# The MLP's tokens in three blocks of 128 and a doubled rest of 64, whose mixing products run as pairs in the row halves

## The chip, the cores and the metric

One core of a Trainium2 chip runs the whole program. Its engines have queues of their own and meet at semaphores: TensorE (PE, with its weight loads as PEld), VectorE (DVE), ScalarE (ACT), GpSimd (POOL) and SyncE (SP), which issues most DMAs. The metric is the device time of one execution in microseconds.

## The reference: what is computed

Three layers on 4 batches of S = 448 tokens with 768 channels:

```
scores = cap * tanh(scale * q @ k.T / cap);  x = softmax(scores) @ v        # 12 heads of 64
out += mask[e] * w[e] * causal_attention(x @ wq[e], x @ wk[e], x @ wv[e]) @ wo[e]   # 4 experts, 2 chosen per token
h = gelu(x @ w_in);  u, v = h[..., :512], h[..., 512:]                       # the MLP
v_n = layer_norm(v) * g_ln
v_s = einsum('ts,bsd->btd', w_sg, v_n) + b_sg                                # mixes the tokens
out = x + (u * v_s) @ w_out
```

The change is in the MLP: in v, its norm, and the mixing product with w_sg over the 448 tokens.

## The kernel before

Products that need more than one pass of precision are made of a high and a low part, rounded to fp32r: hi*hi + hi*lo + lo*hi, three matmuls per slice. A matmul of plain f32 is two records in the trace, one of fp32r a single one (the trace prints f32 for both on PE). The first 48 slots hold the 12 heads of each batch, with the experts of the batch before beside them; there the program order is pinned on every engine (`keep_in_program_order`, and `pin` for PE). Behind them `pe_pin[0] = False`: PE's matmuls of the last part, from some 280 us on, are ordered by the scheduler, by its own estimate of when each can run, and the other engines follow. That last part holds the experts of batch 3 (tiles qk3, a3, pe3, tr3, pt3, v3), the ends of batch 2's (tr2, av2) and the whole MLP, interleaved by `together`:

- `mlp_a(b)` (L858): yh, yl are the high and low part of the MLP's input, channels on partitions (128 x 2 x 448). For each of NC = 4 chunks of CP = 112 tokens, 6 matmuls give hv (tokens x 512 in one PSUM bank); `gelu2` (ACT and DVE, with two buffers of `tmp`) gives vg, DVE takes mean and variance, POOL the power (rstd), and vh, vl (112 x 4 x 512) are the normed v in two parts.
- `mlp_b(b)` (L892): for each f of 4 slices of 128 features, `up(f)` gives u from 6 matmuls hu, and `gate(f)` the mixing sp: 4 chunks x 3 matmuls that contract over 112 tokens each, 448 columns wide; DVE scales and gates it (vs), ACT rounds gh, DVE takes the rest gl.
- `mlp_c(b)` (L936): six slices m of the output o, 18 matmuls each (6 from y, 12 from gh and gl).
- `mlp_weights`: loads and rounds w_sg (sg_h, sg_l, in the same chunks of 112), w_out in thirds, and wo (wo_h, wo_l), wu_h, wu_l.

`tmp` (L806) is a ring of 6 buffers of 128 x 512, `ps` five PSUM banks for hv, hu, sp and o. A matmul whose operands lie in 64 partitions (64*112 and 64*128 in the rows) uses one row half of the array; so do the products a of the experts (two heads, one in each half: a3_0_0_2 and a3_0_1_2 are blocks 2 of heads 0 and 1 of expert pair 0) and s of the attention. av runs in column halves (112*64).

Of the kernel before, what the change touches and what calls it, by code (L numbers as in the profile page):

```python
# [10 lines left out]
F32 = mybir.dt.float32  # L11
# [16 lines left out]
FH = FF // 2  # L28
# [46 lines left out]
def build(ctx: ExitStack, tc: tile.TileContext, a: dict):  # L75
# [44 lines left out]
    def mm(*args, **kw):  # L120
        pin(nc.tensor.matmul(*args, **kw))  # L121
# [669 lines left out]
    w2 = ES(tc.tile_pool(name="w2", bufs=1, side="right", reuse_waits="tile"))  # L791
    ml = ES(tc.tile_pool(name="ml", bufs=1, side="right", reuse_waits="tile"))
    ps = ES(tc.tile_pool(name="ps", bufs=5, space=PSUM, side="right", reuse_waits="tile"))
    sg_h = w3.tile([CP, NC, S], F32R, name="sg_h")
    sg_l = w3.tile([CP, NC, S], F32R, name="sg_l")
    gln = w3.tile([128, 4], F32, name="gln")
    bsg = w3.tile([128, S], F32, name="bsg")
    mhalf = w3.tile([CP, 1], F32, name="mhalf")
    w2_h = w2.tile([128, 2, FF], F32R, name="w2_h")
    w2_l = w2.tile([128, 2, FF], F32R, name="w2_l")  # L800
    wu_h = wp.tile([128, 4, DM], F32R, name="wu_h", tag="wa")
# [2 lines left out]
    wo_l = wp.tile([128, 2, DM], F32R, name="wo_l", tag="wb")  # L804

    def tmp(name):  # L806
        return ml.tile([128, 512], F32, tag="tmp", name=name, bufs=6)

    def mlp_weights(part):
        if part == 1:  # L810
            yield from more_weights()
            return
        if part == 2:
            for i in range(3):
                yield from w_out(3, i, 3, *[lambda dt, name: ml.tile([128, 512], dt, tag="tmp", name=name, bufs=6)] * 2, by="a")
            return
        for k in range(2):
            nc.sync.dma_start(w2_h[:, k, :].bitcast(F32), w2_d[0][:, k, :])
            nc.sync.dma_start(w2_l[:, k, :].bitcast(F32), w2_d[1][:, k, :])
        nc.sync.dma_start(gln, a["g_ln"])  # L820
        nc.sync.dma_start(bsg, a["b_sg"].to_broadcast([128, S]))
        dve.memset(mhalf, -0.5)
        for k in range(NC):
            t = tmp(f"w_sgT{k}")[:CP, :S]
            nc.sync.dma_start(t, a["w_sgT"][:, k, :])
            rnd("pav"[int(GA) % 10], sg_h[:, k, :], t)
            rest("pv"[int(GA) // 10], sg_l[:, k, :], t, sg_h[:, k, :])
        yield 1.0
# [29 lines left out]
    def mlp_a(b):  # L858
        while b == 1 and B - 1 not in X:
            yield 500.0  # L860
        yh, yl = (pool.tile([128, 2, S], F32R, tag=tag, name=f"y{t}{b}", bufs=n)
                  for t, (pool, tag, n) in zip("hl", y_places[b]))
        rnd("v", yh, YA[b])
        rest("p" if YL else "v", yl, YA[b], yh)
        pool, *tags = v_places[b]
        vh = pool.tile([CP, NC, FH], F32R, tag=tags[0], name=f"vh{b}")
        vl = pool.tile([CP, NC, FH], F32R, tag=tags[1], name=f"vl{b}")
        for c in range(NC):
            g = ps.tile([128, 512], F32, tag="g", name=f"hv{b}_{c}")
            n = 0  # L870
            for k in range(2):
                ck = slice(c * CP, (c + 1) * CP)
                for x, w in ((yh, w2_h), (yh, w2_l), (yl, w2_h)):
                    mm(g[:CP, :], x[:, k, ck], w[:, k, FH:], start=(n == 0), stop=(n == 5))
                    n += 1
            yield 1278.0
            vg = tmp(f"vg{b}_{c}")[:CP, :]
            gelu2(vg, g[:CP, :], CP, FH, f"v{b}_{c}")

            bs = ml.tile([CP, 6], F32, tag="bs", name=f"bs{b}_{c}", bufs=2)  # L880
            dve.bn_stats(bs, vg)
            mv = ml.tile([CP, 2], F32, tag="mv", name=f"mv{b}_{c}", bufs=2)
            dve.bn_aggr(mv, bs)
            rstd = ml.tile([CP, 1], F32, tag="rstd", name=f"rstd{b}_{c}", bufs=2)
            dve.tensor_scalar(rstd, mv[:, 1:2], 4e-6, None, op0=ALU.add)
            pool_e.tensor_tensor(rstd, rstd, mhalf, op=ALU.pow)
            dve.tensor_scalar(vg, vg, mv[:, 0:1], rstd, op0=ALU.subtract, op1=ALU.mult)
            rnd("a", vh[:, c, :], vg)
            rest("p" if c < SL else "v", vl[:, c, :], vg, vh[:, c, :])
        st[b] = (yh, yl, vh, vl)  # L890

    def mlp_b(b):  # L892
        yh, yl, vh, vl = st[b]
        pool, *tags = g_places[b]
        gh, gl = ([pool.tile([128, S], F32R, tag=tag, name=f"g{t}{b}_{f}", bufs=4) for f in range(4)]
                  if tag[:2] == "pe" else
                  columns(pool.tile([128, 4, S], F32R, tag=tag, name=f"g{t}{b}"))
                  for t, tag in zip("hl", tags))
        us = {}

        def up(f):
            g = ps.tile([128, 512], F32, tag="g", name=f"hu{b}_{f}")
            n = 0
            fk = slice(f * 128, (f + 1) * 128)
            for k in range(2):
# [92 lines left out]
def _layout(x):  # L998
    q, k, v = x["q"], x["k"], x["v"]
    wide = lambda w: w.transpose(1, 0, 2).reshape(DM, E * HD)  # L1000
    wo = x["moe_wo"].reshape(E * HD, DM)
    out = {
        "qT": q.reshape(B, HP, 2, S, D).transpose(0, 2, 4, 1, 3).reshape(B, 2 * D, HP, S),
        "kT": k.reshape(B, HP, 2, S, D).transpose(0, 2, 4, 1, 3).reshape(B, 2 * D, HP, S),
        "v": v[:, :, :KB * 128].reshape(B, H, KB, 128, D).transpose(0, 3, 1, 2, 4),
        "vt": v[:, :, KB * 128:].reshape(B, HP // 2, 2, 2, KT, D).transpose(0, 1, 2, 4, 3, 5).reshape(B, HP // 2, 2 * KT, 2, D),
        "wqk": _rows(np.concatenate([wide(x["moe_wq"]), wide(x["moe_wk"])], 1)),
        "wvg": _rows(np.concatenate([wide(x["moe_wv"]), x["moe_w_gate"]], 1)),
        "wo": _rows(wo),
        "woT": _rows(wo.T),  # L1010
        "w_in": _rows(x["moe2_w_in"]).view(np.int64),
        "w_out": _rows(x["moe2_w_out"]).view(np.int64),
        "w_sgT": x["moe2_w_sg"].T.reshape(NC, CP, S).transpose(1, 0, 2),
        "g_ln": x["moe2_g_ln"].reshape(4, 128).T,
        "b_sg": x["moe2_b_sg"].reshape(1, S),
    }
# [12 lines left out]
    return {n: np.ascontiguousarray(w) for n, w in out.items()}
# [17 lines left out]
```

## Time and profile before

| | |
|---|---|
| median of 3 runs | 529.7 us (528.77 to 530.01) |
| the profiled execution | 528.26 us |
| its span | 526.5 us |

The page shows busy times, the span in 40 slices, DMA queues, and the chain of work that ended last, followed back from the last instruction. The rows that matter stand below. A duration of a matmul is modelled and overlaps the next one; what one costs in a row of many is the distance from start to start.

### The profile page before, as it was taken

The page shows a single profiled execution, that of the slowest core. Times are in us where ns is not written, and L with a number is a line of the kernel's source. Part 1 is how long each engine was busy: PE and PEld are TensorE (multiplying, and loading weights), DVE is VectorE, ACT ScalarE, POOL GpSimd, SP SyncE. Part 2 cuts the span into 40 slices and gives each one's busy share as a digit, 9 for nine tenths or more (in the row PEclk, how much of TensorE's full clock was granted, in tenths as well). Part 3 has the DMA queues.
Part 4 walks back from the last instruction along what each step waited for, and adds up shares of the span by engine and source line. Part 5 has one row for each costly group of instructions (what it writes and reads, how often), then busy time and mean ns, then how long its engine had stood idle before and what let it go on. Part 6 is the DMA issues. An engine that isn't in the chain of part 4 may idle for free.

```text
span 526.5 us, 7575 instructions
## 1 busy us (share of the span) xinstructions
PE 509.7 (97%) x2726; PEld 333.6 (63%) x2726; DVE 331.0 (63%) x693; ACT 320.8 (61%) x532; POOL 111.7 (21%) x134
## 2 busy tenths in 40 slices
PE   7999999999999999999999999999899999999997
PEld 2233333455655555555466758878778899899996
DVE  4999998974467546465774698838424795483300
ACT  7989899788777776768652675633444363352211
POOL 0000000161451341441340716009030010010000
PEclk9999999999999999999999999999899999999999
DMA  8965529553514232440129312200620001001111
GB/s 317 336 214 162 186 60 244 168 170 112 150 60 149 56 114 84 114 97 13 34 79 269 76 40 71 71 1 12 229 89 17 2 0 54 35 34 38 36 59 63
DMA packets 34693, 54.16 MB, mean 103 GB/s; under 512 B 5536, under 2 KB 29536, under 8 KB 34656
## 3 DMA queue, kind: packets, MB, share of 16 engines
q1 hardware_dynamic: 33936, 50.31, 31.0%
q0 software_dynamic: 576, 3.15, 1.7%
q8 instruction: 21, 0.34, 0.3%
q10 hardware_dynamic: 144, 0.23, 0.1%
q14 instruction: 16, 0.13, 0.1%
HBM read 41.92 MB, written 11.75 MB: 102 GB/s over the span
## 4 chain that ended last, share of the span: by engine, by line
PE 70%; DVE 13%; ACT 6%; DMA 4%; issue 3%; POOL 3%; SPq 1%; DVEq 0%; POOLq 0%; ACTq 0%
PE o L121 16%; PE po L121 8%; PE s L121 8%; PE qk L121 7%; PE sp L121 7%; PE v L121 5%; PE hv L121 4%; ACT p L106 4%; PE a L121 3%; PE hu L121 3%; PE av L121 3%; PE tr L539 3%; DVE pb L106 3%; DMA rb<-rd 2%; POOL pe L106 1%
## 5 line engine op out<-in xcount | busy, mean ns | idle before, releaser
L106 ACT ACTIVATE p<-s,tsc 128x896 f32<-128x896 f32 x84 | 80.9, 1006 | 19.1 <-PE s L121 18.8
L121 PE MATMUL s<-qp,kp 64*128 64x448 f32 (+1 forms) x384 | 78.1, 566 | 2.7 <-ACT p L106 2.7
L106 ACT ACTIVATE p<-p,capt 128x1792 f32<-128x1792 f32 (+1 forms) x48 | 76.9, 1603 | 1.1
L106 DVE TENSOR_TENSOR pb<-pb,p 128x896 f32<-128x896 f32 (+1 forms) x48 | 53.2, 1109 | 19.7 <-ACT p L106 10.5
L106 POOL TENSOR_TENSOR pb<-p 128x896 f32<-128x896 f32 x14 | 29.9, 2134 | 167.1 <-PE po L121 93.5
L121 PE MATMUL po<-p,vv 128*64 128x448 f32 x288 | 59.4, 548 | 0.0
L121 PEld LDWEIGHTS s<-qp,kp 64*128 64x128 f32 (+1 forms) x384 | 27.2, 173 | 47.6 <-issue 24.0
L106 DVE CUSTOM_DVE_ANT_0 a<-a,neg 112x112 f32<-112x112 f32 (+3 forms) x64 | 28.1, 463 | 35.1 <-PE a L121 34.6
L106 POOL TENSOR_SCALAR pe<-pe,cs 112x112 f32<-112x112 f32 (+1 forms) x64 | 37.8, 615 | 57.6 <-DVE cs L106 57.6
L106 ACT ACTIVATE pe<-a,m 112x112 f32<-112x112 f32 (+3 forms) x64 | 31.3, 494 | 19.8 <-DVE m L106 18.3
L121 PEld LDWEIGHTS po<-p,vv 128*64 128x64 f32 x288 | 18.5, 136 | 37.9 <-issue 34.7
L121 PE MATMUL qk<-xh,wqk_h 128*128 128x448 f32 x96 | 37.2, 389 | 0.1
L106 ACT ACTIVATE ob<-o 128x448 f32<-128x448 f32 x24 | 13.0, 541 | 37.8 <-PE o L121 37.8
L121 PE MATMUL o<-gh,wu_h 128*128 128x448 f32 x96 | 35.8, 373 | 0.0
L121 PE MATMUL o<-gl,wu_h 128*128 128x448 f32 x96 | 35.8, 372 | 0.0
L121 PE MATMUL qk<-xh,wqk_l 128*128 128x448 f32 x96 | 35.2, 366 | 0.0
L121 PE MATMUL o<-gh,wu_l 128*128 128x448 f32 x96 | 34.8, 368 | 0.0
L539 PE MATMUL tr<-ident,pe 112*112 112x112 f32 x160 | 25.9, 266 | 6.7 <-ACT pe L106 2.5
L106 POOL TENSOR_TENSOR rstd<-rstd,mhalf 112x1 f32<-112x1 f32 x16 | 10.2, 635 | 102.3 <-DVE rstd L106 98.9
L106 ACT ACTIVATE pt<-tr 112x112 f32<-112x112 f32 (+3 forms) x48 | 18.8, 404 | 17.2 <-PE tr L539 16.9
L121 PE MATMUL v<-wvg_h,xh 128*112 128x260 f32 x96 | 28.5, 296 | 0.1
L539 PEld LDWEIGHTS tr<-ident,pe 112*112 112x112 f32 x160 | 18.3, 135 | 14.5 <-issue 8.8
(228 smaller groups left out, 1097.5 us busy)
## 6 DMA issues: line engine op xcount, KB each, us to landing
rb<-rd SPq DMA_DIRECT2D x24, 224.0 KB, 5.8
out_dram<-ob SPq DMA_DIRECT2D x24, 224.0 KB, 1.9
kp<-in_kT_dram SPq DMA_DIRECT2D x23, 224.0 KB, 3.1
qp<-in_qT_dram SPq DMA_DIRECT2D x23, 224.0 KB, 3.3
vv<-in_v_dram SPq DMA_DIRECT2D x24, 192.0 KB, 3.4
wuw<-in_w_out_dram SPq DMA_DIRECT2D x6, 384.0 KB, 3.4
wud<-wuw SPq DMA_DIRECT2D x12, 192.0 KB, 1.9
ws<-in_wqk_dram SPq DMA_DIRECT2D x4, 384.0 KB, 6.4
```

The lines of the kernel that those rows point to most:

```text
L106: ins = f(*args, **kw)
L121: pin(nc.tensor.matmul(*args, **kw))
L539: pin(nc.tensor.transpose(g[:CP, j * CP:(j + 1) * CP], pe[:, j * CP:(j + 1) * CP], ident))
```

## The change

The tokens are cut into 3 blocks of 128 and a rest of 64 (KB = 3, KT = 64) instead of 4 chunks of 112. The rest is stored twice, in partitions 0 to 63 and 64 to 127. To get v so, the last 64 columns of yh and yl are copied twice side by side into yrh, yrl (DVE, two copies per batch), which are the stationary operand of the fourth hv. w_sg is laid out likewise in DRAM, its last 64 rows twice. The mixing of one f is then 9 matmuls of 128 rows (`mixed`) and three of 64 rows (`rests`), which are issued for f and f + 1 in turns, f in the lower row half and f + 1 in the upper. The gates of f and f + 1 follow both. tmp has 5 buffers instead of 6.

```diff
-    sg_h = w3.tile([CP, NC, S], F32R, name="sg_h")
-    sg_l = w3.tile([CP, NC, S], F32R, name="sg_l")
+    sg_h = w3.tile([128, KB + 1, S], F32R, name="sg_h")
+    sg_l = w3.tile([128, KB + 1, S], F32R, name="sg_l")
...
-        return ml.tile([128, 512], F32, tag="tmp", name=name, bufs=6)
+        return ml.tile([128, 512], F32, tag="tmp", name=name, bufs=5)
...
-        for k in range(NC):
-            t = tmp(f"w_sgT{k}")[:CP, :S]
+        for k in range(KB + 1):
+            t = tmp(f"w_sgT{k}")[:, :S]
...
+        rh, rl = (ml.tile([128, 2, 2, KT], F32R, tag=f"yr{t}", name=f"yr{t}{b}", bufs=1) for t in "hl")
+        for r, y in ((rh, yh), (rl, yl)):
+            dve.tensor_copy(r, y[:, :, KB * 128:].unsqueeze(2).to_broadcast([128, 2, 2, KT]))
+        last = {id(yh): rh, id(yl): rl}
         pool, *tags = v_places[b]
-        vh = pool.tile([CP, NC, FH], F32R, tag=tags[0], name=f"vh{b}")
-        vl = pool.tile([CP, NC, FH], F32R, tag=tags[1], name=f"vl{b}")
-        for c in range(NC):
+        vh = pool.tile([128, KB + 1, FH], F32R, tag=tags[0], name=f"vh{b}")
+        vl = pool.tile([128, KB + 1, FH], F32R, tag=tags[1], name=f"vl{b}")
+        for c in range(KB + 1):
             g = ps.tile([128, 512], F32, tag="g", name=f"hv{b}_{c}")
             n = 0
             for k in range(2):
-                ck = slice(c * CP, (c + 1) * CP)
                 for x, w in ((yh, w2_h), (yh, w2_l), (yl, w2_h)):
-                    mm(g[:CP, :], x[:, k, ck], w[:, k, FH:], start=(n == 0), stop=(n == 5))
+                    ck = (x[:, k, c * 128:(c + 1) * 128] if c < KB else
+                          last[id(x)][:, k].rearrange("p t q -> p (t q)"))
+                    mm(g, ck, w[:, k, FH:], start=(n == 0), stop=(n == 5))
                     n += 1
...
-        def gate(f):
+        def mixed(f):
             g = ps.tile([128, 512], F32, tag="g", name=f"sp{b}_{f}")
-            n = 0
             fk = slice(f * 128, (f + 1) * 128)
-            for c in range(NC):
+            for c in range(KB):
                 for x, w in ((vh, sg_h), (vh, sg_l), (vl, sg_h)):
-                    mm(g[:, :S], x[:, c, fk], w[:, c, :], start=(n == 0), stop=(n == 3 * NC - 1))
-                    n += 1
+                    mm(g[:, :S], x[:, c, fk], w[:, c, :], start=(c == 0 and w is sg_h and x is vh), stop=False)
+            return g
+
+        def rests(gs):
+            for x, w in ((vh, sg_h), (vh, sg_l), (vl, sg_h)):
+                for f, g in gs.items():
+                    r = slice(64 * (f % 2), 64 * (f % 2) + 64)
+                    mm(g[:, :S], x[r, KB, f * 128:(f + 1) * 128], w[r, KB, :], start=False, stop=x is vl)
+
+        def gate(f, g):
...
-        for f in range(4):
-            if f < 3:
-                up(f + 1)
-                yield 1120.0
-            gate(f)
-            yield 2240.0
+        for f in (0, 2):
+            gs = {}
+            for t in (f, f + 1):
+                if t < 3:
+                    up(t + 1)
+                    yield 1120.0
+                gs[t] = mixed(t)
+                yield 1830.0
+            rests(gs)
+            for t, g in gs.items():
+                gate(t, g)
+            yield 610.0
```

The scheduler lays out PE's last part anew from this. Three places of its order, each as it stands before and after. Number behind a name: the instruction's own.

PE in batch 0, where the mixing of f = 2 ends, before (sp0_2 is the mixing of batch 0, f = 2; tr are transposes of the experts):

```order
L121 MATMUL sp0_2_3315<-sg_h_2483,vh0_2551 128x448
L121 MATMUL sp0_2_3315<-sg_l_2484,vh0_2551 128x448
L121 MATMUL sp0_2_3315<-sg_h_2483,vl0_2552 128x448
L121 MATMUL a3_0_0_0_3072<-qk3_0_2979 112x112
L121 MATMUL a3_0_1_0_3073<-qk3_0_2979 112x112
L539 MATMUL tr2_1_1_0_3095<-ident_73,pe2_1_1_0_2852 112x112
L121 MATMUL a3_0_0_0_3072<-qk3_0_2979 112x224
L121 MATMUL a3_0_1_0_3073<-qk3_0_2979 112x224
L121 MATMUL sp0_3_3388<-sg_h_2483,vh0_2551 128x448
```

and after; the last three sp0_2 rows here are its three half-row products:

```order
L121 MATMUL sp0_2_3315<-sg_h_2483,vh0_2555 128x448
L121 MATMUL sp0_2_3315<-sg_l_2484,vh0_2555 128x448
L121 MATMUL sp0_2_3315<-sg_h_2483,vl0_2556 128x448
L539 MATMUL tr2_1_1_1_3094<-ident_73,pe2_1_1_1_2864 112x112 x2
L539 MATMUL tr2_1_1_2_3111<-ident_73,pe2_1_1_2_2913 112x112 x3
L121 MATMUL sp0_3_3353<-sg_h_2483,vh0_2555 128x448
```

The halves of sp0_2 stand alone behind its nine full products, and those of sp0_3 stand alone behind its own.

PE in batch 3's experts, before (a3 are score blocks of two heads, av2 the products of batch 2's probabilities with v, v3 the projection of v):

```order
L121 MATMUL hv1_3_3636<-w2_h_2488,yl1_3537 112x512
L121 MATMUL a3_0_0_2_3147<-qk3_0_2979 112x336
L121 MATMUL a3_0_1_2_3148<-qk3_0_2979 112x336
L121 MATMUL av2_1_3159<-pt2_1_0_3013,vp2_2393 64x448
L121 MATMUL av2_1_3159<-pt2_1_1_3094,vp2_2393 64x448
L121 MATMUL av2_1_3159<-pt2_1_0_3013,vp2_2393 64x336
L121 MATMUL av2_1_3159<-pt2_1_1_3094,vp2_2393 64x336
L121 MATMUL av2_1_3159<-pt2_1_0_3013,vp2_2393 64x224
L121 MATMUL av2_1_3159<-pt2_1_1_3094,vp2_2393 64x224
L121 MATMUL av2_1_3159<-pt2_1_0_3013,vp2_2393 64x112
L121 MATMUL av2_1_3159<-pt2_1_1_3094,vp2_2393 64x112
L121 MATMUL v3_1_3187<-wvg_h_77,xh3_2895 112x260
```

and after, where a3_0_0_2 stands in v3_0 and a3_0_1_2 in hv1_1, further up:

```order
L121 MATMUL av2_1_3165<-pt2_1_0_3017,vp2_2393 64x448
L121 MATMUL av2_1_3165<-pt2_1_1_3090,vp2_2393 64x448
L121 MATMUL av2_1_3165<-pt2_1_0_3017,vp2_2393 64x336
L121 MATMUL v3_1_3175<-wvg_h_77,xh3_2899 112x260
L121 MATMUL av2_1_3165<-pt2_1_1_3090,vp2_2393 64x336
L121 MATMUL av2_1_3165<-pt2_1_0_3017,vp2_2393 64x224
L121 MATMUL av2_1_3165<-pt2_1_1_3090,vp2_2393 64x224
L121 MATMUL av2_1_3165<-pt2_1_0_3017,vp2_2393 64x112
L121 MATMUL a3_0_0_3_3195<-qk3_0_2983 112x448
L121 MATMUL av2_1_3165<-pt2_1_1_3090,vp2_2393 64x112
L121 MATMUL v3_1_3175<-wvg_l_78,xh3_2899 112x260
```

The two a's have left each other, and av2_1 is cut into three pieces, by a v3_1 product and by a3_0_0_3.

PE in batch 3's first mixing group, before (o2 are output products of batch 2):

```order
L121 MATMUL sp3_1_4493<-sg_h_2483,vh3_4249 128x448
L121 MATMUL sp3_1_4493<-sg_l_2484,vh3_4249 128x448
L121 MATMUL sp3_1_4493<-sg_h_2483,vl3_4250 128x448
L121 MATMUL sp3_1_4493<-sg_h_2483,vh3_4249 128x448
L121 MATMUL sp3_1_4493<-sg_l_2484,vh3_4249 128x448
L121 MATMUL sp3_1_4493<-sg_h_2483,vl3_4250 128x448
L121 MATMUL o2_2_4467<-gh2_4025,wu_h_2490 128x448
L121 MATMUL o2_2_4467<-gl2_4026,wu_h_2490 128x448
```

and after, where the rows sp3 here are all half-row products; a first one of sp3_0 stands 28 rows further up between o2_1 and o2_2:

```order
L121 MATMUL o2_2_4488<-gh2_4037,wu_l_2491 128x448
L121 MATMUL sp3_1_4495<-sg_h_2483,vh3_4262 128x448
L121 MATMUL sp3_0_4447<-sg_l_2484,vh3_4262 128x448
L121 MATMUL o2_3_4520<-yh2_3931,wo_h_2492 128x448
L121 MATMUL o2_3_4520<-yl2_3932,wo_h_2492 128x448
L121 MATMUL o2_3_4520<-yh2_3931,wo_l_2493 128x448
L121 MATMUL sp3_1_4495<-sg_l_2484,vh3_4262 128x448
L121 MATMUL sp3_0_4447<-sg_h_2483,vl3_4263 128x448
L121 MATMUL sp3_1_4495<-sg_h_2483,vl3_4263 128x448
L121 MATMUL o2_3_4520<-yh2_3931,wo_h_2492 128x448
```

The six half-row products of this group stand in three places.

## Rows read from the trace of the kernel before

**Rows 1.** The page, part 1: busy us (share of the span) xinstructions of each engine.

```profile
PE 509.7 (97%) x2726; PEld 333.6 (63%) x2726; DVE 331.0 (63%) x693; ACT 320.8 (61%) x532; POOL 111.7 (21%) x134
```

**Rows 2.** Stretches: from:to, length; PE, PEld, DVE, ACT, POOL busy (instructions); PEclk, DMA share, GB/s.

```profile
320.00:380.00 60.00, 57.27 (x320) 47.12 (x318) 40.49 (x109) 29.32 (x76) 19.34 (x30) 0.97 0.24 80
380.00:440.00 60.00, 60.00 (x307) 50.06 (x306) 33.74 (x69) 27.50 (x56) 7.28 (x12) 1.00 0.08 28
...
340.00:350.00 10.00, 10.00 (x70) 7.14 (x69) 5.09 (x13) 4.42 (x12) 0.55 (x1) 1.00 0.01 2
```

**Rows 3.** The chain that ended last: start us, us, what.

```profile
31.26 3.63 PE w2ps L121 x8
...
416.35 5.57 PE hv L121 x24
...
442.59 2.43 PE sp L121 x12
...
497.49 25.16 PE o L121 x123
```

**Rows 4.** Timeline of the attention: start, us, engine, instruction, count, idle before.

```profile
148.26 1.77 PE L121 MATMUL s<-qp,kp 64*128 64x448 f32 x8
...
149.12 0.19 PEld L121 LDWEIGHTS s<-qp,kp 64*128 64x128 f32 x2 [0.18 <-issue]
```

**Rows 5.** Timeline of PE around a single a product between o products.

```profile
384.92 0.37 PE L121 MATMUL o<-gh,wu_h 128*128 128x448 f32 x1
385.21 1.00 PE L121 MATMUL a<-qk 64*112 64x448 f32 x2
...
386.45 0.37 PE L121 MATMUL o<-gh,wu_l 128*128 128x448 f32 x1
```

**Rows 6.** Timeline of PE from the last hv of batch 1 on.

```profile
343.57 0.82 PE L121 MATMUL a<-qk 64*112 64x336 f32 x4
344.32 2.11 PE L121 MATMUL av<-pt,vp 112*64 112x448 f32 x16
346.36 0.37 PE L121 MATMUL v<-wvg_h,xh 128*112 128x260 f32 x1
...
348.01 0.28 PE L121 MATMUL v<-wvg_l,xh 128*112 128x260 f32 x1
...
349.37 0.28 PE L121 MATMUL v<-wvg_h,xh 128*112 128x260 f32 x1
```

**Rows 7.** Timeline of the stall at 370 us and behind it.

```profile
369.95 0.55 POOL L106 TENSOR_TENSOR rstd<-rstd,mhalf 112x1 f32<-112x1 f32 x1 [0.79 <-DVE rstd L106]
...
371.74 0.47 PE L539 MATMUL tr<-ident,pe 112*112 112x112 f32 x3 [1.85 <-ACT pe L106]
...
373.79 0.57 PE L121 MATMUL o<-gl,wu_h 128*128 128x448 f32 x1
...
374.16 0.57 PE L121 MATMUL o<-gh,wu_h 128*128 128x448 f32 x1
```

**Rows 8.** The stretches there, columns as in Rows 2: PEclk is third from the end.

```profile
372.00:374.00 2.00, 2.00 (x11) 1.84 (x9) 0.98 (x3) 1.74 (x5) 0.00 (x0) 0.78 1.08 414
374.00:376.00 2.00, 2.00 (x9) 1.46 (x10) 0.55 (x1) 0.11 (x1) 0.00 (x0) 0.50 1.04 402
376.00:378.00 2.00, 2.00 (x10) 1.28 (x11) 1.01 (x4) 0.83 (x2) 0.00 (x0) 0.87 0.09 31
```

**Rows 9.** Timeline of DVE ahead of the stall: the gating, then a gelu.

```profile
360.86 0.52 DVE L106 TENSOR_TENSOR cs<-cs,wt 112x4 f32<-112x4 f32 x2
...
363.73 0.69 DVE L106 SCALAR_TENSOR_TENSOR vg<-gsv,hv 112x512 f32<-112x512 f32 x1 [0.75 <-POOL pe L106]
```

**Rows 10.** Groups of instructions by form: count, busy us, mean ns, idle before.

```profile
L121 PEld LDWEIGHTS sp<-sg_h,vh 112*128 112x128 f32 x64 | 12.0, 188 | 2.3 <-ACT pe L106 0.7 <-ACT vh L106 0.5 <-issue 0.3
...
L106 DVE SCALAR_TENSOR_TENSOR vs<-sp,gln,bsg 128x448 f32<-128x448 f32 x16 | 10.9, 681 | 18.0 <-PE sp L121 18.0
...
L106 DVE TENSOR_SCALAR wum<-wum 128x256 int32<-128x256 int32 x6 | 1.6, 282 | 0.0
```

More of the change, by code (lines that the diff above doesn't have):

```diff
@@ L793, in build @@
     ps = ES(tc.tile_pool(name="ps", bufs=5, space=PSUM, side="right", reuse_waits="tile"))
-    sg_h = w3.tile([CP, NC, S], F32R, name="sg_h")
-    sg_l = w3.tile([CP, NC, S], F32R, name="sg_l")
+    sg_h = w3.tile([128, KB + 1, S], F32R, name="sg_h")
+    sg_l = w3.tile([128, KB + 1, S], F32R, name="sg_l")
     gln = w3.tile([128, 4], F32, name="gln")
     bsg = w3.tile([128, S], F32, name="bsg")
-    mhalf = w3.tile([CP, 1], F32, name="mhalf")
+    mhalf = w3.tile([128, 1], F32, name="mhalf")
     w2_h = w2.tile([128, 2, FF], F32R, name="w2_h")
@@ L814, in mlp_weights @@
             for i in range(3):
-                yield from w_out(3, i, 3, *[lambda dt, name: ml.tile([128, 512], dt, tag="tmp", name=name, bufs=6)] * 2, by="a")
+                yield from w_out(3, i, 3, *[lambda dt, name: ml.tile([128, 512], dt, tag="tmp", name=name, bufs=5)] * 2, by="a")
             return
@@ L871, in mlp_a @@
             for k in range(2):
-                ck = slice(c * CP, (c + 1) * CP)
                 for x, w in ((yh, w2_h), (yh, w2_l), (yl, w2_h)):
-                    mm(g[:CP, :], x[:, k, ck], w[:, k, FH:], start=(n == 0), stop=(n == 5))
+                    ck = (x[:, k, c * 128:(c + 1) * 128] if c < KB else
+                          last[id(x)][:, k].rearrange("p t q -> p (t q)"))
+                    mm(g, ck, w[:, k, FH:], start=(n == 0), stop=(n == 5))
                     n += 1
             yield 1278.0
-            vg = tmp(f"vg{b}_{c}")[:CP, :]
-            gelu2(vg, g[:CP, :], CP, FH, f"v{b}_{c}")
-            bs = ml.tile([CP, 6], F32, tag="bs", name=f"bs{b}_{c}", bufs=2)
+            vg = tmp(f"vg{b}_{c}")
+            gelu2(vg, g, 128, FH, f"v{b}_{c}")
+            bs = ml.tile([128, 6], F32, tag="bs", name=f"bs{b}_{c}", bufs=2)
             dve.bn_stats(bs, vg)
-            mv = ml.tile([CP, 2], F32, tag="mv", name=f"mv{b}_{c}", bufs=2)
+            mv = ml.tile([128, 2], F32, tag="mv", name=f"mv{b}_{c}", bufs=2)
             dve.bn_aggr(mv, bs)
-            rstd = ml.tile([CP, 1], F32, tag="rstd", name=f"rstd{b}_{c}", bufs=2)
+            rstd = ml.tile([128, 1], F32, tag="rstd", name=f"rstd{b}_{c}", bufs=2)
             dve.tensor_scalar(rstd, mv[:, 1:2], 4e-6, None, op0=ALU.add)
@@ L1012, in _layout @@
         "w_out": _rows(x["moe2_w_out"]).view(np.int64),
-        "w_sgT": x["moe2_w_sg"].T.reshape(NC, CP, S).transpose(1, 0, 2),
+        "w_sgT": np.concatenate([x["moe2_w_sg"].T, x["moe2_w_sg"].T[KB * 128:]]).reshape(KB + 1, 128, S).transpose(1, 0, 2),
         "g_ln": x["moe2_g_ln"].reshape(4, 128).T,
```

## The prediction

> **What bounds the kernel now.** I read the page's busy times first: TensorE (PE) is busy 97% of the span [rows 1], so a change to PE's work counts wherever nothing else is late. The table by stretches shows where that is: from 380 to 440 us PE is busy 60.00 of 60.00 us; from 320 to 380 it is 57.27 of 60.00 [rows 2]. The chain of waits agrees: in the last third it lies almost only on PE's rows, among them the mixing products sp and the v halves hv, and it ends with 25.16 us of o [rows 3]. So the unit of the sum is PE's step, the distance of two starts, not the modelled duration. An sp step is 2.43/12 = 0.203 us; an hv step 5.57/24 = 0.232; an o step, which contracts 128 rows where sp contracts 112, is 25.16/123 = 0.205 [rows 3]. Rows of contraction cost nothing; matmuls do.
>
> **The mixing: fewer slots, more switches.** Before, each of 4 batches x 4 f issues 12 sp steps, 192 in all. After, 9 full ones per f (144, at the same 0.203) and 3 half-row ones of 64 rows (48). So 48 x 0.203 = 9.74 us of steps are replaced by halves.
>
> What a half costs: no half-row matmul of this type (fp32r) is in the trace. The nearest are s in the attention, f32, in row halves 64*128: 8 records take 1.77 us, and their weight loads come in twos, 0.19 long with 0.18 of idle time before them, so every 0.37 us a pair [rows 4]. Two halves share one load time and one step. A full-array f32 record of 512 columns takes 3.63/8 = 0.45, 0.40 for 448 [rows 3]. So a pair costs no more than one full-array matmul of its type; for fp32r I take 0.203 per pair, and 0.203 for a half alone. The upper bound is two steps per pair (rival below).
>
> What a group costs at its edges: the single a products of the experts (half rows, f32) stand between o products. From the o at 384.92 to the second o behind the a, 386.45, there are 1.53 us; two o steps are 0.41 and two f32 records 0.74, so one excursion into the row halves and back costs 0.38. Between v products the same: 348.01 to 349.37 is 1.36, less two v steps of 0.12 and 0.74: 0.38 [rows 5, 6]. I take 0.19 per switch; the lower bound is 0, since between 112 and 128 rows there is none.
>
> Were every group of two f's together, it would be 8 groups: 24 x 0.203 + 8 x 0.38 = 7.91, a gain of 1.83 us. The order shows less. In batch 0, f2 and f3 run their three halves alone, each in its own excursion (6 slots, 2 excursions). In batch 1 the first group is cut by the av2/av3 products (one excursion more). In batch 3 the first is cut into three (4 slots, 3 excursions). Five groups are whole. That is 20 pairs + 8 singles = 28 slots, 11 excursions: 28 x 0.203 + 11 x 0.38 = 5.68 + 4.18 = 9.86 against 9.74. **Term: +0.1.** The halving is eaten by the switches.
>
> **What the new order does to its neighbours.** Before, a3_0_0_2 and a3_0_1_2 stand side by side behind hv1_3, then the eight av2_1 in one run, then v again: four records of a and sixteen of av end by 346.36 [rows 6]. After, one a lies between v3_0 products, the other between hv1_1 products, and av2_1 is cut by a v3_1 and by a3_0_0_3. Switches there: 10 against 5, 5 x 0.19 = 0.95. The two a's lose their partner: 2 f32 records of 336 columns, 0.37 x 336/448 = 0.28 each, 0.56. The av pieces of 448, 336, 224 and 112 columns ran as pairs (0.74 + 0.56 + 0.37 + 0.19 = 1.86, seen as about 2 us [rows 6]); cut, the first 336 runs alone and the next pairs with a 224: 0.56 more. **Term: +2.1.** PE is busy 10.00 of 10.00 from 340 to 350 [rows 2], so nothing covers it.
>
> **The stall at 370.** PE waits 1.85 us before 371.74 for ACT's pe [rows 7]; its clock, granted 1.00 before, falls to 0.78, 0.50 and 0.87 in three stretches of 2 us (full is 2.4 GHz, 0.50 is 1.2) [rows 8], where an o steps by 0.37 (373.79 to 374.16) [rows 7]. 6 us at a mean of 0.72 lose 1.7 us more. Does the +2.1 vanish in this wait? I think not: what is late behind it hangs on PE too. The gating (cs on DVE, 360.86) waits for the last v3 products; POOL's scalings of pe3_0 and the gelus follow, a vg waits 0.75 for one of them [rows 9]; so all shift with PE. The change also puts rstd1_0 on POOL behind wo's rounding and all eight pe3_0 scalings, with the wu_h and wu_l transfers queued behind it (one pow, 0.55 us, later [rows 7]); and with five buffers of tmp the vg1 chain stands behind the gates of batch 0, while o0_1 to o0_4 wait for vg1 to free PSUM. These push the stall up, a shorter a-path in DVE's order pulls it down. **Term: 0**, bounds -3.5 (stall and dip go, 1.85 + 1.7) and +2 (twice the stall).
>
> **At no cost.** hv stays at 24 steps a batch, and its loads of 128 columns take the 188 ns of sp's, under a step of 0.232 [rows 3, 10]. The copies yrh, yrl: eight on DVE, each about one wum TENSOR_SCALAR of 128x256 (0.28) [rows 10]; 2.3 us, hidden by PE's work, as DVE is busy 33.74 of 60 us behind 380 [rows 2]; uncovered they would cost all of it. vg, gs and the statistics have 128 partitions instead of 112 and the same length. The gates now wait for two f's: a wait moved behind the rests, with DVE's vs and ACT's gh queued behind. A gate is three operations on DVE and one on ACT, of 0.68 at most like the vs [rows 10], 2.7, two in a row under 5.4; behind the last rests of batch 3 stand 32 steps, 6.5 us, before an o needs gh3_2. w_sgT is loaded in 4 x 224 KB instead of 196, well ahead. a3_1_0_0's pair is cut by a tr (two switches) next to the stall: taken as 0, bound +0.4.
>
> Sum: +0.1 + 2.1 + 0 = +2.2 on the profiled run's 528.26, 530.5; the median of the runs is 1.4 higher, so **531.9**.
>
> **A rule weighed.** All loads here run under a matmul on the same rows of the array: an sp load is 0.188 long in a step of 0.203 [rows 3, 10]. The Trainium skill, "TensorE: Matmul & The Clock Gate", Part 3 (packing small matmuls), says under what overlaps that a weight load overlaps a matmul in flight only when the row groups differ; by it the halves that run alone would pay for their loads, rival (e). The sp rows, full array behind full array, contradict it.
>
> **The rivals.**
> (a) The stall and the dip go. A later PE may find ACT's pe ready: the gap is 1.85, about the +2.1. It decides if that pe comes no later than before, at about 371.7. Against it: the chain through the gating. 531.9 - 3.5 = 528.4, 18%.
> (b) A part is absorbed or cheaper: only the stall's 1.85 is filled, or an excursion into fp32r halves costs half (11 x 0.19 = 2.1 less): 529.8 to 530.1, 26%.
> (c) The stall grows: with five tmp buffers and the pow moved, vg1_0 comes later than o0_1 can hide; it decides once the chain is over 2 us later, PE's delay: 533.9 (+2), 8%.
> (d) The halves do not run side by side, the change doesn't do what it says: 20 pairs take 40 slots, +4.1: 536.0, 4%.
> (e) The eight halves that run alone each show their load of 0.188: 8 x 0.188 = 1.5 more, 533.4, 2%.
>
> **How the numbers follow.** The forecast itself (530.9 to 533.2) has 42%. A measurement can tell about 0.2% (1.1 us) from no change: same is 528.6 to 530.8. Faster: (a), 18%. Same: (b), 26%. Slower: forecast, (c), (d) and (e), 56%. The range runs from 528.4, the middle of (a), to 534.5, beyond (c) with some spread; out are half of (a) and (d), some 14%.
>
> **What would show it.** In the profile after: rests of a whole group at six starts in three steps of about 0.20, with some 0.1 us more at either edge; if a pair steps by 0.4, (d). Around 343 to 350, a of 64x336 in twos, not fours, and av in pieces. At 370, the wait for ACT's pe and the granted clock below 1.00 behind it: gone in (a), over 3 us in (c). From 380 on, PE without gaps and shorter by about 0.4 us: batches 1 to 3 have 19 slots and 8 excursions, 6.9 us, for 36 steps, 7.3. I am wrong if the switches into fp32r halves cost far from 0.38, or if other work than PE sets 340 to 380.

## The result, and the profile after

The changed kernel takes 533.8 us (median of 5 runs, 532.77 to 534.42); the kernel before, beside it, 530.01. The ratio is 1.0078, 95% interval 1.0051 to 1.0105: slower by 2.7 to 5.6 us. The prediction was 531.9, range 528.4 to 534.5, slower with 56%. Sign and range held, the size was too small; the section on why the prediction was right shows which of its terms hold and which do not.

The page of the changed kernel, part 1, as [rows 1]: busy us (share of the span) and instructions.

```profile
PE 512.2 (96%) x2726; PEld 328.7 (62%) x2726; DVE 333.9 (63%) x701; ACT 320.3 (60%) x532; POOL 110.7 (21%) x134
```

PE has as many records as before (2726) and 2.5 us more busy time. The span is 531.1 us against 526.5, so the rest of the 4.6 us is time in which PE waits. 1.6 us of that lie ahead of the part that the change concerns: the first hv waits 2.74 us for the load of w2, against 1.17. What PE waits for from 300 us on, in the table of waits (us in total, times, longest):

```profile
PE tr L539 <- ACT pt L106: 2.3, 4, 1.1
PE hu L121 <- DVE u L106: 0.8, 1, 0.8
PE o L121 <- DVE vg L106: 0.4, 1, 0.4
PE tr L539 <- ACT pe L106: 0.3, 1, 0.3
```

The same table of the kernel before (its second profile, c_before below):

```profile
PE tr L539 <- ACT pe L106: 1.8, 1, 1.8
PE tr L539 <- POOL pe L106: 0.9, 1, 0.9
PE tr L539 <- ACT pt L106: 0.8, 2, 0.5
```

The one long wait for pe [rows 7] is gone, the 0.9 us for POOL too; the waits for pt have grown from 0.8 to 2.3, and waits for u and vg have come.

Three parts of the new order, as the prediction asked for them. The halves of one f alone (timeline of PE in batch 0), which answers [rows 5]:

```profile
337.24 0.36 PE L121 MATMUL sp<-sg_l,vh 128*128 128x448 f32 x1
337.44 0.37 PE L121 MATMUL sp<-sg_h,vl 128*128 128x448 f32 x1
337.74 0.47 PE L121 MATMUL sp<-sg_h,vh 64*128 64x448 f32 x1
338.05 0.36 PE L121 MATMUL sp<-sg_l,vh 64*128 64x448 f32 x1
338.25 0.36 PE L121 MATMUL sp<-sg_h,vl 64*128 64x448 f32 x1
338.54 0.51 PE L121 MATMUL hv<-w_h,yh 128*128 128x512 f32 x1
338.88 0.39 PE L121 MATMUL hv<-w_l,yh 128*128 128x512 f32 x1
```

A step inside is 0.20, as of a full product. The excess stands at the edges: 0.09 (337.44 to 337.74), 0.11, 0.08 and, on the first hv, 0.34 instead of 0.23: 0.39 in all, where 0.38 was taken. And a whole group, in batch 1:

```profile
419.35 0.37 PE L121 MATMUL sp<-sg_h,vl 128*128 128x448 f32 x1
419.64 0.47 PE L121 MATMUL sp<-sg_h,vh 64*128 64x448 f32 x2
419.96 0.37 PE L121 MATMUL sp<-sg_l,vh 64*128 64x448 f32 x2
420.16 0.37 PE L121 MATMUL sp<-sg_h,vl 64*128 64x448 f32 x2
420.46 0.51 PE L121 MATMUL hv<-w_h,yh 128*128 128x512 f32 x1
```

Two records (x2) share a row: the pairs do run side by side, three steps for six halves. In batch 3's experts the a's stand apart and av2_1 is cut, against one run each in [rows 6]:

```profile
344.07 0.82 PE L121 MATMUL a<-qk 64*112 64x336 f32 x2
...
348.51 1.53 PE L121 MATMUL av<-pt,vp 112*64 112x448 f32 x6
...
350.29 1.16 PE L121 MATMUL av<-pt,vp 112*64 112x336 f32 x8
351.37 1.00 PE L121 MATMUL a<-qk 64*112 64x448 f32 x2
352.31 0.41 PE L121 MATMUL av<-pt,vp 112*64 112x112 f32 x2
```

### The profile page after: what moved, and what is told of

Its sections match the earlier page's. It is cut to its first block, busy times and chain, and to the rows that moved or that the text cites. A ratio compares the mean times of both kernels' runs of the same rounds, so it can differ in the third digit from the quotient of the medians.

```text
span 531.1 us, 7584 instructions
## 1 busy us (share of the span) xinstructions
PE 512.2 (96%) x2726; PEld 328.7 (62%) x2726; DVE 333.9 (63%) x701; ACT 320.3 (60%) x532; POOL 110.7 (21%) x134
## 3 DMA queue, kind: packets, MB, share of 16 engines
q0 software_dynamic: 576, 3.15, 1.7%
## 4 chain that ended last, share of the span: by engine, by line
PE 74%; DVE 11%; DMA 6%; ACT 5%; issue 2%; SPq 1%; POOL 0%; DVEq 0%; ACTq 0%
PE o L121 16%; PE po L121 9%; PE s L121 9%; PE qk L121 7%; PE sp L121 7%; PE v L121 6%; PE hv L121 4%; PE a L121 4%; PE av L121 4%; PE hu L121 3%; ACT p L106 3%; PE tr L539 2%; DMA rb<-rd 2%; DVE pb L106 2%; PE sum L121 2%
## 5 line engine op out<-in xcount | busy, mean ns | idle before, releaser
L106 POOL TENSOR_SCALAR pe<-pe,cs 112x112 f32<-112x112 f32 (+1 forms) x64 | 36.1, 584 | 55.6 <-DVE cs L106 55.6
L106 POOL TENSOR_TENSOR rstd<-rstd,mhalf 128x1 f32<-128x1 f32 x16 | 10.6, 665 | 84.6 <-DVE rstd L106 82.7
L121 PE MATMUL a<-qk 64*112 64x112 f32 (+3 forms) x128 | 27.5, 430 | 0.6 <-ACT qk L106 0.6
```

The costliest lines, as they stand in the source:

```text
L106: ins = f(*args, **kw)
```

## How two profiles are compared here

Each row of PE in a trace can be given the instruction's place in the program, since the order on PE is fixed. So the start of, say, the last product of hv1_0 can be set beside the same one in another profile. Done for two profiles of the changed kernel (after and c_after), everything behind the last product of hu0_0 agrees within 0.07 us. Ahead of it, where the loads of w2 and the early loads set the time, the last product of hu0_0 starts anywhere from 300.4 to 305.2 us (e_tmp6, below, apart). All differences below are therefore counted from there on, in us, against c_before. The column names are those of the experiments.

| start of the last product of | after | e_gather | e_nosplit | e_both | e_full | e_tmp5 | e_split |
|---|---|---|---|---|---|---|---|
| qk3_0_0 (batch 0, before the mixing) | +0.55 | +0.50 | +0.54 | +0.54 | +0.52 | 0.00 | 0.00 |
| qk3_0_1 (behind the mixing of f = 0, 1) | -0.84 | -0.88 | -0.84 | -0.85 | -0.58 | -1.10 | 0.00 |
| hu0_3 | +0.26 | +0.21 | +0.66 | +0.18 | +0.04 | -0.64 | 0.00 |
| hv1_0 (behind the mixing of f = 2, 3) | +1.52 | +0.87 | +1.91 | +0.84 | +0.56 | +0.49 | 0.00 |
| v3_3 (behind the a and av2_1) | +2.99 | +2.33 | +1.42 | +0.32 | +2.02 | +0.49 | +1.96 |
| hu1_1 (behind the stall) | +3.84 | +3.15 | +2.25 | +1.14 | +2.85 | +1.80 | +1.96 |
| hv2_3 (end of batch 1's mixing) | +3.73 | +2.84 | +2.13 | +0.83 | +3.19 | +1.80 | +1.96 |
| hv3_3 (end of batch 2's) | +3.31 | +2.52 | +1.72 | +0.49 | +3.19 | +1.80 | +1.96 |
| o3_5 (the end) | +3.94 | +2.25 | +2.34 | +0.22 | +3.32 | +1.80 | +1.96 |

The change's part is +3.94 us at the end, which agrees with the medians (3.8 here, 4.6 in the repeat c_after).

## The experiments

In the kernels e_nosplit, e_gather, e_both, e_full, e_tmp5, e_split, e_tmp6, e_dupsame, e_dupboth and e_bothact the order on PE from the first hv on is written out as a list and chained, so that one thing can be moved without a new plan of the scheduler. e_full has the changed kernel's list unaltered, and in its trace ACT, DVE and POOL run in the changed kernel's order too. Where the list or the buffers are altered, the scheduler gives DVE and ACT a somewhat different order (in e_tmp5 from 315 us on). The edits of the order are shown as parts of that list, shortened, with a name and the number of its matmuls. In these kernels line 121 is L141 and 539 is L559.

```diff
+    def impose(order):      # tile names with counts: "sp0_2:9 hu0_3:6 ..."
+        for t in want:
+            ins = queues[t].pop(0)
+            if last is not None:
+                tc.add_manual_dep(ins, last.name, ..., reason="order")
+            last = ins
```

**c_after** and **c_before**: both kernels once more, unaltered.

> The changed kernel once more, unaltered, for the part of the difference that only one profile shows. In the profile on record the first hv waits 2.7 us for the load of w2 where the kernel before waits 1.2, and the span is 0.6 us longer before the MLP begins. Theory (PE's order sets the time): both are the variation of transfers between runs, so this profile shows another wait, between 1.0 and 3.0, and its time is 533.8 +- 1. Rival (the change delays the load): 2.7 +- 0.2 again.

> The kernel before once more, unaltered. In the profiles so far everything behind the first u product (hu0_0) agrees to some 0.05 us between two executions of one kernel, and from there to the end the changed kernel takes 2.3 us more. Ahead of it, where loads set the time, the changed kernel and its variants reach hu0_0 between 300.7 and 304.7 us, the one profile of before at 300.4. Theory (loads vary between executions, the change has no part in it): before reaches hu0_0 at 300.4 to 304 as well in this profile. Rival (the change makes the stretch ahead longer, by 1.5 to 2 us as the medians say): 300.4 +- 0.5 again.

c_after: 533.83 us, ratio 1.0083 (1.0051 to 1.0115); c_before 529.37, ratio 1.0005 (0.9982 to 1.0028). c_after waits 2.1 us for the load of w2 (2.7 in the first profile) and reaches the last product of hu0_0 at 303.9. c_before waits 2.7 us there and reaches it at 303.8, not 300.4: the loads vary as much in one kernel, and no part of the change shows in them. But c_before shows something that the expectation didn't ask for. The timeline of its stall, as [rows 7], and the stretches, as [rows 8] (PEclk is third from the end):

```profile
375.10 0.47 PE L539 MATMUL tr<-ident,pe 112*112 112x112 f32 x3 [1.82 <-ACT pe L106]
```

```profile
374.00:376.00 2.00, 0.91 (x6) 0.91 (x7) 1.58 (x6) 1.81 (x9) 0.00 (x0) 1.00 1.11 433
376.00:378.00 2.00, 2.00 (x14) 1.66 (x13) 1.29 (x2) 1.10 (x3) 0.00 (x0) 1.00 1.07 418
378.00:380.00 2.00, 2.00 (x12) 1.43 (x12) 1.04 (x4) 1.13 (x4) 0.00 (x0) 1.00 0.70 266
```

The stall is there with 1.82 us, and the granted clock stays at 1.00 (2.4 GHz) behind it; against the first profile of before this alone is 1.60 us. But c_before has its own dip, 90 us earlier, behind the 2.73 us in which PE stands idle for the load of w2 (stretches of c_before):

```profile
280.00:282.00 2.00, 0.00 (x0) 0.00 (x0) 1.02 (x4) 1.34 (x4) 0.00 (x0) 0.99 0.79 183
282.00:284.00 2.00, 1.55 (x4) 1.22 (x5) 0.00 (x0) 0.00 (x0) 0.00 (x0) 0.50 1.11 235
284.00:286.00 2.00, 2.00 (x11) 1.79 (x10) 1.17 (x2) 0.00 (x0) 0.00 (x0) 0.65 1.01 244
```

It loses 1.7 us of clock there, as much as the first profile loses behind the stall. Ten of the fourteen profiles show such a fall to 0.50 behind that load, after a wait of 2.0 to 3.1 us; before alone (wait 1.17) has it at 373, and e_gather (1.11), e_tmp5 (1.38) and after (2.74) have none. So the dip is no accident of one execution, but it isn't bound to the stall at 370 either: it comes behind the one wait or the other, or not at all. For the comparison this means that before has it inside the stretch counted here and c_before ahead of it. Against before the change looks like 2.3 us from hu0_0 on, against c_before like 3.94.

**e_nosplit**: the a's and av2_1 in one run.

```diff
-  hv1_3 x5, av2_1 x3, v3_1, av2_1 x4, a3_0_0_3, av2_1, v3_1 ...   (a3_0_0_2 in v3_0, a3_0_1_2 in hv1_1)
+  hv1_3 x5, a3_0_0_2, a3_0_1_2, av2_1 x8, v3_1, a3_0_0_3, v3_1 ...
```

> The changed kernel with its own order on PE written out, but a3_0_0_2, a3_0_1_2 and the eight av2_1 side by side again, where av2_1 begins. Theory (switches and lost partners cost what was summed): 5 switches x 0.19 + 0.56 + 0.56 = 2.1 us less between the end of sp0_3 and the end of v3_3; time about 531.7 if nothing behind waits instead. Rival (ring of five tmp buffers sets 340 to 400 us): the stretch shrinks, the wait behind 367 us grows by the same, time as the changed kernel, 533.8.

532.36 us, 1.0054 (1.0029 to 1.0080). From hv1_0 to v3_3 it takes 1.96 us less than the changed kernel (1.91 to 1.42, against 1.52 to 2.99), as summed; ahead of that hu0_3 waits 0.4 longer for DVE's u. This is not the edit's doing: up to there all engines run in the changed kernel's order, but ACT's gelu waits 1.79 us for a store of wuw, where it waits 1.38 in the changed kernel (rows at e_tmp5). The stall does not grow, so the rival falls. The whole, 1.60 less.

**e_split**: the kernel before with that split.

```diff
-  hv1_3, a3_0_0_2, a3_0_1_2, av2_1 x8, v3_1 x14, a3_0_0_3 ...
+  v3_0 x8, a3_0_0_2, v3_0 x5, a3_0_1_2, v3_0 x5, av2_1 x3, hv1_3, v3_1, av2_1 x4, a3_0_0_3, av2_1, v3_1 ...
```

> The kernel before with its own order on PE written out, but a3_0_0_2 and a3_0_1_2 each alone among v3_0 products and av2_1 cut into 3, 4 and 1 by a v3_1 and a3_0_0_3, as in the changed kernel. Theory: 5 switches and the lost partners cost 2.1 us between the end of sp0_3 and the end of v3_3 also here; time about 531.3 against 529.2. Rival (the cost shown by the repaired order belongs to something else of the change): under 1 us.

533.22 us, 1.0060 (1.0034 to 1.0087). In the trace exactly +1.96 appears between hv1_0 and v3_3 and stays to the end; elsewhere the column is 0.00. The term of the prediction (2.1) is shown from both sides, as a sum; what the switches and what the lost partners cost was not taken apart. The median rises by more, 3.2 us by the ratio: the profile of e_split loses 3.4 us of clock at 281 to 289 us, ahead of the stretch counted here, where c_before loses 1.7, and eight of its twelve executions have a mean granted clock of 0.992 or 0.993. Why these are more often there than in the kernel before is open.

**e_gather**: the half products of two f side by side.

```diff
-  sp0_2 x9, sp0_2 x3 (halves), tr..., sp0_3 x9, sp0_3 x3 (halves)          (and the cut groups in batches 1 and 3)
+  sp0_2 x9, tr..., sp0_3 x9, (sp0_2, sp0_3) x3 (halves)
```

> The changed kernel with its own order on PE written out, but the six half-row products of every two f side by side, at the place of the last of them. 24 slots instead of 28 and 68 switches in the last part instead of 75. Theory: 4 x 0.203 + 7 x 0.19 = 2.1 us less; time about 531.7. Rival (halves of one f alone are hidden behind DVE's and ACT's work in batch 0, and gates come later when they are gathered): under 1 us less, 532.8 to 534.

531.59 us, 1.0041 (1.0017 to 1.0066); 1.69 us less than the changed kernel in the trace: 0.65 in batch 0, 0.20 in batch 1 and 0.90 in batch 3 (0.63 lost there becomes 0.27 won). Close to the 2.1 from counting; the rival (under 1 us) falls.

**e_full**: no halves.

```diff
-                    r = slice(64 * (f % 2), 64 * (f % 2) + 64)
+                    r = slice(0, 128)
```

> The changed kernel with its own order on PE written out, but the three products of the rest contract over all 128 rows, so no row half is used and no switch is made for them; the rest's tokens are counted twice so. Theory (28 slots and 11 excursions cost as much as 48 full steps): 9.7 us against 9.9, so the stretch from hu0_0 to the end changes by -0.1, +-0.4. Rival (halves save their 4 us and the loss is elsewhere): 2 to 4 us more.

533.54 us, 1.0067 (1.0036 to 1.0097); 0.62 us less than the changed kernel in the trace. By place: the mixing of f = 0, 1 is 0.29 worse without halves, hu0_3 waits 0.48 less, the mixing of f = 2, 3, where each f's halves stand alone, is 0.74 better (0.52 against 1.26), and from hu1_1 to the end it is 0.37 worse. The 0.48 at hu0_3 is not the halves': ACT's gelu ahead of it waits 0.90 us for a store of wuw here, 1.38 in the changed kernel. Without it the kernel is 0.14 us faster without halves, where 0.1 was expected. All told, halves in this order gain nothing; the rival, that they save 4 us, falls.

Since the order is the same on every engine, this pair of kernels also shows what the halves do at each place, beside what the prediction's counting (0.203 per slot, 0.19 per switch) gives:

| the halves in | won, measured | won, counted |
|---|---|---|
| batch 0, f = 0, 1 | +0.29 | +0.23 |
| batch 0, f = 2, 3 (each f alone) | -0.74 | -0.76 |
| batch 1 | +0.45 | +0.46 |
| batch 2 | +0.42 | +0.46 |
| batch 3 | -0.50 | -0.50 |

**e_tmp5**: the kernel before with five buffers, its order on PE kept.

```diff
-        return ml.tile([128, 512], F32, tag="tmp", name=name, bufs=6)
+        return ml.tile([128, 512], F32, tag="tmp", name=name, bufs=5)
```

> The kernel before with its own order on PE written out and five tmp buffers instead of six; nothing else. Rival theory (the buffer taken away delays ACT and DVE): hu0_3 waits for u and tr for pt, 1 to 2 us more between hu0_0 and the end of qk3_1_1, 530.2 to 531.2. Theory (order only): within 0.5 us of 529.2.

531.69 us, 1.0027 (1.0002 to 1.0053); +1.80 in the trace. The theory "only PE's order" is refuted. The rival's size holds, its place does not: up to qk3_1_1 it is 0.49, and 1.31 come behind it, at the stall. One buffer less, with the order that the scheduler then gives DVE and ACT, costs about as much as the split. The waits of PE from 300 us on:

```profile
PE tr L559 <- ACT pe L106: 1.6, 1, 1.6
PE sp L141 <- DVE u L106: 0.9, 1, 0.9
PE tr L559 <- ACT pt L106: 0.8, 2, 0.5
PE o L141 <- DVE rstd L106: 0.5, 1, 0.5
PE o L141 <- DVE vg L106: 0.4, 1, 0.4
PE hu L141 <- DVE u L106: 0.2, 1, 0.2
```

Beside those of before stand waits for u (the gelu of the same slice, 1.1), rstd and vg (0.9): these are the chains that take buffers of tmp. How the ring holds them is seen in the changed kernel, on ACT in batch 0:

```profile
327.34 0.55 ACT L106 ACTIVATE gsu<-hu 128x448 f32<-128x448 f32 x1 [1.38 <-DMA wud<-wuw]
328.57 0.58 ACT L106 ACTIVATE gsu<-gsu 128x448 f32<-128x448 f32 x1 [0.69 <-DVE gsu L106]
```

and on PE behind it:

```profile
329.86 0.47 PE L121 MATMUL hu<-yh,w_h 128*128 128x448 f32 x1 [0.83 <-DVE u L106]
```

The first step of a gelu waits 1.38 us until a buffer is stored that w_out's conversion holds (wuw); then u, which reads its slice from PSUM, is late, and hu0_3 waits 0.83 for it. In c_before, with six buffers, no first step of a gelu in this batch waits for such a store. In the profiles with a longer or shorter wait for the store (1.79 in e_nosplit, 0.90 in e_full) hu0_3 waits 1.23 and 0.34: it follows the store.

**e_tmp6**: six buffers, the copies in one of them.

```diff
-        rh, rl = (ml.tile([128, 2, 2, KT], F32R, tag=f"yr{t}", name=f"yr{t}{b}", bufs=1) for t in "hl")
+        yr = ml.tile([128, 512], F32R, tag="tmp", name=f"yr{b}", bufs=6)...
+        rh, rl = yr[:, 0], yr[:, 1]
```

> The changed kernel with its own order on PE written out, and six tmp buffers as before: the copies yrh and yrl take one buffer of that ring while mlp_a needs them, instead of 2 kB of their own. Rival theory (the ring of five delays ACT and DVE): the wait of hu0_3 for DVE's u (0.8 us) and part of the waits for ACT's pt (2.8 us) go, 1 to 2 us less, 532 to 533. Theory (only PE's order): no change, 533.8 +- 0.5.

537.51 us, 1.0159 (1.0130 to 1.0187), slower by far, and neither theory's number. The copies of batch 0 run at 288.41 us instead of 276.89, behind other work of DVE that waits for DMAs, and the first hv of the fourth block waits for them:

```profile
288.72 0.79 PE L141 MATMUL hv<-w_h,yr 128*128 128x512 f32 x1 [5.85 <-DVE yr L106]
```

That their place in the ring put them there is likely, but no run shows what they waited for. Counted from hu0_0 on, as in the table, the kernel says something on the ring after all: with the same order on PE and six buffers it stands at +1.11 at the end, 2.83 less than the changed kernel, and neither the 0.55 before the mixing nor the wait of hu0_3 is there (0.00 at qk3_0_0, -1.38 at hu0_3). But PE comes some 6 us later there and DVE and ACT have that much of a start, so this is no price of the ring. Its copies of batch 1 do not run at 302 us any more but at 348, with no instruction on POOL from 345 to 352:

```profile
348.75 0.28 DVE L106 CAST yr<-yh 128x256 fp32r<-128x256 f32 x1
348.95 0.29 DVE L106 CAST yr<-yl 128x256 fp32r<-128x256 f32 x1
```

**e_both**: both repairs of the order, the edits of e_nosplit and e_gather together.

> The changed kernel with its own order on PE written out and both repairs: the half-row products of every two f side by side, and a3_0_0_2, a3_0_1_2 and av2_1 in one run; five tmp buffers. Theory now (three causes that add up: the split of a and av 2.0 us, the scattered halves 1.7, the fifth tmp buffer 1.8): from hu0_0 to the end 3.2 to 3.6 us less than the changed kernel, still 0.4 to 0.8 more than the kernel before; time about 530.3 where before is 529.4. Rival (repairs overlap, since DVE and ACT are late either way): 1.5 to 2.5 less.

529.62 us, 1.0002 (0.9976 to 1.0029): level with before. 3.72 us less than the changed kernel; +0.22 against before. Slightly more than the two single repairs (3.29), because the longer wait of hu0_3 in e_nosplit does not occur. The rival (repairs overlap) falls. With both repairs the halves should win 1.8 by counting, and the fifth buffer should cost 1.80 by e_tmp5: that they cancel fits the 0.22, but was not shown apart.

**e_dupsame** and **e_dupboth**: six buffers without copies on DVE, the doubled block made by DMA; in the changed kernel's order and with both repairs.

```diff
-                    ck = (x[:, k, c * 128:(c + 1) * 128] if c < KB else last[id(x)]...)
+                    ck = slice(c * 128 - p0, c * 128 - p0 + 128)          # p0 = 64 for the fourth, else 0
...
+            if c == KB:
+                nc.sync.dma_start(vh[:KT, c, :].bitcast(F32), vh[KT:, c, :].bitcast(F32))
+                nc.sync.dma_start(vl[:KT, c, :].bitcast(F32), vl[KT:, c, :].bitcast(F32))
```

> The changed kernel with its own order on PE written out, six tmp buffers, and no copies yrh, yrl: the fourth hv takes the last 128 tokens, only its upper 64 rows are kept, and vh's and vl's last block is copied from partitions 64 to 127 into 0 to 63 by two DMAs per batch. Theory now: the waits of hu0_3 for u and of tr for pt in batch 0 shrink, 1.5 to 2 us less than the changed kernel from hu0_0 to the end; 532. Rival (order only): 0 +- 0.4. Third way: the two DMAs come late and PE waits for vh, more than the changed kernel.

> As e_dupsame, with both repairs of the order. Theory now: all three causes are gone, what is left is the halves' own 1.8 us of gain less some of it in batch 0: from hu0_0 to the end 1 to 1.5 us less than the kernel before in its undisturbed profile; 528.2 where before is 529.4. Rival (halves gain nothing even so): as before, 529.4 +- 0.5.

534.58 us, 1.0116 (1.0081 to 1.0151), and 532.30, 1.0042 (1.0010 to 1.0074): neither theory's number but the third way. PE waits for the two copies in batch 0 (e_dupsame):

```profile
325.02 0.47 PE L141 MATMUL sp<-sg_h,vh 64*128 64x448 f32 x2 [1.13 <-DMA vh<-vh]
326.83 0.47 PE L141 MATMUL sp<-sg_h,vl 64*128 64x448 f32 x2 [1.14 <-DMA vl<-vl]
```

What the ring alone costs inside the changed kernel is thus not isolated. One thing is: at qk3_0_0 both kernels stand at 0.00, as e_tmp6 does, whose copies of batch 1 run later. All kernels with these two copies at 300 to 304 us stand at +0.50 to +0.55.

**e_bothact**: e_both with the copies on ACT.

```diff
-            dve.tensor_copy(r, y[:, :, KB * 128:].unsqueeze(2).to_broadcast([128, 2, 2, KT]))
+            act.activation(r, y[:, :, KB * 128:]...to_broadcast([128, 2, 2, KT]), AF.Copy)
```

> As e_both (both repairs of the order, five tmp buffers), but the eight copies yrh and yrl run on ACT instead of DVE. On DVE the two of batch 1 took 0.97 and 1.24 us at 302 us and the transposes behind them waited 0.55 us longer than in the kernel before; the kernels without copies on DVE (e_tmp5, e_dupsame) do not show that 0.55. Theory: the 0.55 us go, and from hu0_0 to the end it takes 0.3 us less than the kernel before in its undisturbed profile (e_both: 0.2 more); time 528.6 to 529.4, not to be told from before. Rival (the 0.55 belongs to the 128-row tiles or to ACT): 0.2 more again, or worse since ACT's transposes pt stand behind the copies.

529.04 us, 0.9994 (0.9970 to 1.0019), level with before; +0.25 at the end. The theory falls: at qk3_0_0 it is +0.54 as in e_both, now with tr behind ACT's pe and pt. Of the rival, the 128-row tiles are not the cause, since e_tmp6 and e_dupsame have them too and stand at 0.00; the copies at that place are, on whichever of the two engines they stand. The wait of hu0_3 for u is gone (-0.84 there, e_both +0.18), and is lost again by hv3_3 (+0.52, e_both +0.49). Moving the copies moves the wait. No version here beats the kernel before by more than can be measured.

## Why the prediction was right, and where it was not

Against c_before, in the order of the sum:

- **The halves and their edges** (forecast +0.1). Step 0.20, pairs side by side, 0.39 per excursion, loads hidden: as taken. Rival (d) is refuted by the x2 rows, rival (e), with the rule of the Trainium skill behind it, by 0.20 steps of halves alone. The counts held too, place by place (table at e_full): the halves cost 0.08 in all where 0.1 was counted, and from hu1_1 to the end they save 0.37 where 0.4 was forecast. Against c_before batch 1 won only 0.11; e_full, without halves, loses 0.34 in the same stretch, so that difference is not the halves' but the new order's, which has two transposes (tr3_1_1_1) behind hu1_1 that stood before it. The prediction names one excursion more in batch 1 and leaves it out of its 11; the switches in the order come to 22, so 11 is right.
- **The split of a and av** (forecast +2.1): 1.96, shown by undoing and by doing it. This was the largest term and it was right.
- **The stall at 370** (forecast 0, bounds -3.5 and +2): from qk3_1_1 to hu1_1 the changed kernel loses 0.85. The long wait [rows 7] is cut into 0.39, 0.50, 0.29 and 0.45, 1.63 in all against 1.82, and a3_1_0_0's pair is cut by a tr, whose 0.4 was taken as hidden. That the stall doesn't swallow the +2.1 was right: v3_3's +2.99 is still there behind it. Rival (c) named the cause in part: e_tmp5 loses 1.31 in the same stretch.
- **"At no cost"** is the step that failed. Before the mixing, 0.55; at hu0_3, 1.10. The tmp buffer was looked at only for the stall at 370, and the cover of DVE's work only behind 380 [rows 2]; from 300 to 320 us DVE is busy 18.09 of 20 us in the trace of before, and PE waits for what comes from it. In the kernel before, e_tmp5 puts the buffer's price at 1.80; in the changed kernel hu0_3's wait follows a store of w_out's buffer (e_tmp5, rows), and its price there is not isolated. The 0.55 belongs to the two copies of batch 1: it is gone without them (e_dupsame) and with them later (e_tmp6), and stays with them on ACT (e_bothact). The copies were priced by a row of 0.28 [rows 10], and six of the eight do take 0.28 to 0.34. The two of batch 1 don't (timeline of DVE, then POOL):

```profile
302.06 0.97 DVE L106 CAST yrh<-yh 128x256 fp32r<-128x256 f32 x1 [0.99 <-PE hv L121]
302.95 1.24 DVE L106 CAST yrl<-yl 128x256 fp32r<-128x256 f32 x1
```

```profile
300.59 4.61 POOL L106 TENSOR_TENSOR sg_l<-w_sgT,sg_h 128x448 fp32r<-128x448 f32 x4 [3.65 <-ACT sg_h L106]
```

  They stand beside POOL's four roundings of w_sg and take 3 to 4 times as long. The Trainium skill, "SBUF — State Buffer", in the section on its two separate sides, says that GpSimd and certain VectorE operations share a pair of ports, which the one that starts first holds for its whole instruction while the other waits. The rows fit that: the same two copies take 0.28 and 0.29 us in e_tmp6, with POOL idle. That it is the port and nothing else of POOL's work, no run here shows.
- **Not in the sum: a gain.** The group of f = 0, 1 in batch 0 wins 1.39 (qk3_0_0 to qk3_0_1), not 0.23. The 0.9 us that tr waited for POOL's pe is gone. e_tmp5 and e_full, both without halves, win 1.10 there, so most of it is the new sequence on the other engines, and the pairs have 0.29.

So +2.2 was forecast, and +3.94 came against c_before. The wait terms left out (0.55 + 1.10 + 0.85 = 2.5) outweigh the gain left out (1.2 more than counted); 0.35 more lie in the order of batch 1. Against the profile that the prediction read, the change is +2.34 from hu0_0 on, close to the forecast, but that is luck: that profile has its dip of the clock inside the stretch, worth 1.60. Rival (a) was priced with 1.7 us of clock behind the stall, which a repeat of the same kernel loses at another place.

## What to carry to other kernels

Half-array pairs save steps only if both halves are adjacent and the array is not switched for few of them: three pairs save three steps, 0.6 us, and their excursion costs 0.39, so a group torn in two saves nothing and one whose halves run alone loses. Pin such groups: here the scheduler scattered them and split their neighbours too, and putting both back was worth 3.72 us. A buffer taken from a ring to make room is a term of the sum of its own, to be priced at every stretch where the engines that use the ring are full. And before a stretch of one profile enters a sum, see whether it is the kernel's or that execution's: a second profile tells, if it is read from its start to its end.

## What was not expected of the hardware

The same stall, 1.85 and 1.82 us long, at the same place of the program, was followed in one execution by a granted clock of 0.78, 0.50 and 0.87 for 6 us and in the other by 1.00. The other had lost as much clock, 1.7 us, behind a wait of 2.73 us some 90 us earlier. Nor does the length of a wait tell alone: behind the 2.74 us for w2 in the first profile of the changed kernel the clock stays at 1.00, behind 2.01 us in e_dupsame it falls to 0.50. And a copy of 128x256 on DVE took 0.28 us or 1.24 us, by what ran on POOL beside it.
